# Linear attention with an RMS norm, then a two-layer token MLP: 512-token windows across batches in place of 576-token batches

## The chip, the cores and the metric

The kernel runs on one core of a Trainium2 chip. The metric is the device time of one execution in microseconds (us). The profile covers the same core: TensorE as two rows, PE for matmuls and PEld for weight loads; VectorE (DVE), ScalarE (ACT), GpSimd (POOL) and SyncE (SP). All of q, k, v and both weight matrices are loaded through POOL's DMA queue, which converts float32 to float16 on the way; the output leaves through SP's queue.

## The reference

```python
# q, k, v: (8, 8, 576, 64); w_in: (512, 2048); w_out: (2048, 512); alpha: (2048,)
kv  = np.einsum('bhsd,bhse->bhde', k, v)
out = np.einsum('bhsd,bhde->bhse', q, kv)
rms = np.sqrt(np.mean(out * out, axis=-1, keepdims=True) + 1e-06)
attn = out / rms * g_norm                                  # per head of 64
x = attn.transpose(0, 2, 1, 3).reshape(4608, 512)
h = x @ w_in
g = np.maximum(h, 0.0) + alpha * np.minimum(h, 0.0)
return g @ w_out                                           # (4608, 512) float32
```

The sum over tokens in `kv` does not depend on the order of the tokens, as long as k and v have the same one. In all later steps a token is a column (or a row of the output) on its own.

## The kernel before, in words

Heads are taken in four pairs j, so that two heads of 64 fill 128 partitions. A batch has 576 tokens: four full tiles of 128 and one of 64, whose other half is zeroed once per buffer (L82). There are three buffers each of k, v and q (`ksb`, `vsb`, `qsb`), tokens on partitions.

`load_heads` (L89) loads one tensor of one batch with five DMAs, a tile of 128 tokens each; every piece of a row that it reads is one head's 64 values. Batch 0 is loaded in two halves of four heads, so 30 DMAs; then come `w_in` in four quarters (L133), batch 1, `w_out` in four quarters (L142) and batch 2. All of them are issued by POOL in this order, and the identity matrix for the transposes is made on POOL too (in a library file, masks.py), after the first 30. Each later batch is loaded while the batch two before it is worked on.

Attention of one batch and one pair is four steps:
- `step_t`: five PE transposes of q (`qt_ps`, L180) and a DVE copy to `qt_sb` (L189).
- `step_kv`: five matmuls (`kv_ps`, L196) and a DVE multiplication by a mask that keeps the two heads apart (`kv_sb`, L204).
- `step_ot`: `ot_ps` = kv times q, two matmuls of 288 columns (L209); ACT squares it (`sq_sb`, L214), DVE copies it to `ot_sb` (L216).
- `step_ssq`: a matmul with the mask sums the squares of each head (`ssq_ps`, L222); ACT makes `lnv` = Ln (L227) and `rstd` = Exp (L232); DVE makes `xt` = `ot_sb` x g x `rstd` (L233).

`step_stream` puts them in the order ot(j-1), t(j), ssq(j-1), kv(j), so 16 steps per batch. `qt_ps` and `kv_ps` share one PSUM bank, `ot_ps` and `ssq_ps` one buffer of two banks.

`m1_group(b, g)` makes 128 of the 2048 hidden values for the 576 tokens of batch b: eight matmuls of 288 columns (L276) into `h_ps`, two buffers of two banks each; ACT makes `m_sb` = relu(-h) (L286), and DVE `gt` = h + (1 - alpha) x `m_sb` in float16 (L287). The output product (`y_mm`, L296) is 16 matmuls of 512 columns for each of 36 tiles of 128 tokens; ACT copies the result (`y_out`, L303) and SP stores it.

The order of each engine is the order in which the code is written (manual schedule). First all of batch 0's attention, then its 16 hidden groups, then the output of the first four tiles at once, in four accumulators (`ya` and `yb`, two banks each, in `h_ps`' buffers) with one attention step of batch 1 after each g. From then on, per batch b and g: a hidden group, some output matmuls of earlier tokens (four or five, so that a tile may end and the next begin in the middle of a run), one attention step of the next batch. These output tiles have one PSUM bank (`y_ps`). Batch 1 has no output work, as no complete tile is left. After batch 7 five tiles remain.

Of the kernel before, what the change touches and what calls it, by code (L numbers as in the profile page):

```python
# [9 lines left out]
FP32 = mybir.dt.float32  # L10
# [7 lines left out]
def kernel(  # L18
# [31 lines left out]
    qkv_p = ctx.enter_context(tc.tile_pool(name="qkv", bufs=1))  # L50
    attn_p = ctx.enter_context(tc.tile_pool(name="attn", bufs=2))
# [7 lines left out]
    ctx.enter_context(tc.manual_schedule(engines={ENG.PE, ENG.Activation, ENG.DVE, ENG.Pool, ENG.SP}))  # L59
# [13 lines left out]


# [3 lines left out]
    for i in range(NBUF):  # L78
        t = {}
        for nm in ("k", "v", "q"):  # L80
            t[nm] = qkv_p.tile([P, NT, H, D], FP16, name=f"{nm}sb{i}")
            nc.vector.memset(t[nm][REM:P, NFULL, :, :], 0.0)  # L82
        bufs.append(t)

    def load_heads(b, nm, h0, h1):
        t = bufs[b % NBUF][nm]
        for ti in range(NT):
            n = P if ti < NFULL else REM
            nc.gpsimd.dma_start(  # L89
                out=t[0:n, ti, h0:h1, :],  # L90
                in_=srcs[nm][b, h0:h1, ti * P : ti * P + n, :].rearrange("h s d -> s h d"),
            )
# [16 lines left out]
    ident = const_p.tile([P, P], FP32, name="ident")
    make_identity(nc, ident[:])  # L110
    ident16 = const_p.tile([P, P], FP16, name="ident16")
    nc.vector.tensor_copy(out=ident16[:], in_=ident[:])
    eps_t = const_p.tile([P, 1], FP32, name="eps_t")
    nc.vector.memset(eps_t[:], 1e-6)

    mask32 = const_p.tile([P, P], FP32, name="mask32")
    nc.vector.memset(mask32[:], 0.0)
    nc.vector.memset(mask32[0:64, 0:64], 1.0)
    nc.vector.memset(mask32[64:128, 64:128], 1.0)
    mask16 = const_p.tile([P, P], FP16, name="mask16")  # L120
    nc.vector.tensor_copy(out=mask16[:], in_=mask32[:])
# [8 lines left out]
    def load_w_in():  # L130
        for i in range(WQ):
            t = w_p.tile([P, NC, FW], FP16, name=f"w_in_sb{i}")
            nc.gpsimd.dma_start(  # L133
                out=t[:],
                in_=moe_w_in[:, i * FW : (i + 1) * FW].rearrange("(c p) f -> p c f", p=P),
            )
            w_in_sb.append(t)

    def load_w_out():
        for i in range(WQ):  # L140
            t = w_p.tile([P, GW, D_MODEL], FP16, name=f"w_out_sb{i}")
            nc.gpsimd.dma_start(  # L142
# [245 lines left out]
```

## Time and profile before

| | us |
|---|---|
| Median of 3 runs (378.38 to 378.71) | 378.6 |
| The profiled execution, whole | 378.55 |
| Its span in the profile | 376.4 |
| PE busy (2049 matmuls) | 300.3 |
| DVE busy | 175.1 |
| ACT busy | 167.9 |
| POOL busy | 116.4 |

In timelines and groups a row names the engine, the line of the code, the operation, output <- inputs, the shape (partitions x elements) and a count; what stands in brackets is the idle time just before it and what ended it. Matmuls are pipelined: a row's duration includes the drain, and the cost in a row of matmuls is the distance between starts. `<-issue` means that nothing in the profile explains the wait.

### The profile page before, as it was taken

Reading aid. Unit: us, or ns where it says so; the run is one execution under the profiler, and the core shown is the slowest. Engines: PE = TensorE matmul, PEld = TensorE weight load, DVE = VectorE, ACT = ScalarE, POOL = GpSimd, SP = SyncE. Lnnn points to the kernel's source line nnn. Section 1 sums busy time; section 2 is a strip of 40 time slices with the busy share of each in tenths; the row PEclk is TensorE's granted clock in tenths of the full one; section 3 lists DMA queues with packets and bytes.
Section 4 is the critical chain, followed back from the end, with each engine's and each line's share of the span. In section 5 each row is a group of like instructions: output and inputs, shape, how many; then the busy total and the mean of one; then the engine's idle time right before and its main releaser. Section 6 shows DMA issues by size and latency. Waiting matters only on the chain.

```text
span 376.4 us, 5119 instructions
## 1 busy us (share of the span) xinstructions
PE 300.3 (80%) x2049; PEld 191.0 (51%) x2049; DVE 175.1 (47%) x272; ACT 167.9 (45%) x261; POOL 116.4 (31%) x149
## 2 busy tenths in 40 slices
PE   0033489895886899979997889799978999799885
PEld 0022367443664555556665555566655555466432
DVE  2014348433776544546664454555654455344100
ACT  1003346245666354546664454546553445444211
POOL 8995947939308400290048000000000000000000
PEclk9999999998999999999999999999999999999999
DMA  9999999999909900298059401000000000010111
GB/s 59 81 101 197 154 205 161 154 92 128 174 0 86 132 30 28 42 152 81 29 58 162 56 28 57 28 28 30 30 29 28 30 28 30 28 57 28 50 63 57
DMA packets 122375, 28.13 MB, mean 75 GB/s; under 512 B 113632, under 2 KB 117744, under 8 KB 122352
## 3 DMA queue, kind: packets, MB, share of 16 engines
q0 software_dynamic: 116976, 18.36, 66.1%
q1 hardware_dynamic: 5376, 9.45, 6.7%
q8 instruction: 16, 0.26, 0.3%
q14 instruction: 7, 0.06, 0.0%
HBM read 36.71 MB, written 9.44 MB: 123 GB/s over the span
## 4 chain that ended last, share of the span: by engine, by line
PE 71%; ACT 13%; DVE 7%; POOL 6%; issue 3%; ACTq 0%; POOLq 0%
PE h_ps L276 30%; PE y_ps L296 29%; ACT y_sb L303 4%; ACT lnv L227 4%; DVE xt L233 3%; ACT rstd L232 3%; PE ot_ps L209 3%; PE qt_ps L180 2%; PE ssq_ps L222 2%; POOL ksb L89 2%; POOL vsb L89 2%; POOL qsb L89 2%; PE kv_ps L196 2%; DVE ot_sb L216 1%; ACT m_sb L286 1%
## 5 line engine op out<-in xcount | busy, mean ns | idle before, releaser
L276 PE MATMUL h_ps<-xt,w_in_sb 128*128 128x288 f16 x1024 | 149.6, 292 | 14.9 <-DVE xt L233 12.1
L287 DVE SCALAR_TENSOR_TENSOR gt<-m_sb,beta_sb,h_ps 128x576 f16<-128x576 f32 x128 | 104.0, 813 | 78.1 <-ACT m_sb L286 77.9
L296 PE MATMUL y_ps<-w_out_sb,gt 128*128 128x512 f16 x512 | 128.9, 379 | 13.6 <-ACT y_sb L303 13.6
L286 ACT ACTIVATE m_sb<-h_ps 128x576 f32<-128x576 f32 x128 | 83.0, 648 | 103.5 <-PE h_ps L276 103.5
L276 PEld LDWEIGHTS <-w_in_sb 128*128 128x128 f16 x1024 | 100.2, 100 | 45.0 <-issue 17.1
L296 PEld LDWEIGHTS <-gt 128*128 128x128 f16 x576 | 55.9, 98 | 61.9 <-issue 16.9
L89 POOL DMA_DIRECT2D ksb<-in_k_dram x45 | 37.0, 859 | 78.5 <-PE kv_ps L196 76.7
L233 DVE SCALAR_TENSOR_TENSOR xt<-ot_sb,g2col,rstd 128x576 f16<-128x576 f32 x32 | 26.2, 819 | 46.4 <-ACT rstd L232 46.4
L214 ACT ACTIVATE sq_sb<-ot_ps 128x576 f16<-128x576 f32 x32 | 20.8, 651 | 55.9 <-PE ot_ps L209 55.9
L89 POOL DMA_DIRECT2D vsb<-in_v_dram x45 | 37.0, 872 | 10.6 <-DMA w_out_sb<-in_moe_w_out_dram 6.1
L89 POOL DMA_DIRECT2D qsb<-in_q_dram x45 | 37.2, 905 | 0.2
L216 DVE COPY ot_sb<-ot_ps 128x576 f32<-128x576 f32 x32 | 24.2, 758 | 23.6 <-ACT sq_sb L214 23.6
L227 ACT ACTIVATE lnv<-ssq_ps,eps_t 128x576 f32<-128x576 f32 x32 | 23.7, 742 | 21.4 <-PE ssq_ps L222 21.4
L303 ACT COPY y_sb<-y_ps 128x512 f32<-128x512 f32 x32 | 18.7, 584 | 23.1 <-PE y_ps L296 23.1
L209 PE MATMUL ot_ps<-qt_sb,kv_sb 128*128 128x288 f16 x64 | 14.2, 306 | 12.2 <-DVE kv_sb L204 12.2
L232 ACT ACTIVATE rstd<-lnv 128x576 f32<-128x576 f32 x32 | 21.8, 682 | 1.0
L162 PE MATMUL alpha_ps<-ident,alpha_row 16*128 16x16 f32 x1 | 0.3, 281 | 23.6 <-POOL ident masks.py:199 23.6
L222 PE MATMUL ssq_ps<-sq_sb,mask 128*128 128x288 f16 x64 | 14.0, 302 | 5.7 <-DVE ot_sb L216 5.7
L189 DVE COPY qt_sb<-qt_ps 128x576 f16<-128x576 f16 x32 | 14.4, 451 | 4.8 <-PE qt_ps L180 4.8
L180 PEld LDWEIGHTS <-qsb 128*128 128x128 f16 x160 | 12.8, 105 | 7.4 <-issue 0.8
L196 PEld LDWEIGHTS <-ksb 128*128 128x128 f16 x160 | 12.6, 104 | 7.3 <-issue 0.9
L180 PE MATMUL qt_ps<-ident,qsb 128*128 128x128 f16 x160 | 15.6, 233 | 0.8 <-DVE beta_sb L168 0.8
(28 smaller groups left out, 69.6 us busy)
## 6 DMA issues: line engine op xcount, KB each, us to landing
out_dram<-y_sb SPq DMA_DIRECT2D x36, 256.0 KB, 2.0
ksb<-in_k_dram POOLq DMA_DIRECT2D x28, 128.0 KB, 4.5
vsb<-in_v_dram POOLq DMA_DIRECT2D x28, 128.0 KB, 5.9
qsb<-in_q_dram POOLq DMA_DIRECT2D x28, 128.0 KB, 5.6
w_in_sb<-in_moe_w_in_dram POOLq DMA_DIRECT2D x4, 512.0 KB, 8.2
w_out_sb<-in_moe_w_out_dram POOLq DMA_DIRECT2D x4, 512.0 KB, 10.3
ksb<-in_k_dram POOLq DMA_DIRECT2D x15, 64.0 KB, 3.3
vsb<-in_v_dram POOLq DMA_DIRECT2D x15, 64.0 KB, 3.3
```

Source lines behind the costliest of these rows:

```text
L89: nc.gpsimd.dma_start(out=t[0:n, ti, h0:h1, :], in_=srcs[nm][b, h0:h1, ti * P : ti * P + n, :].rearrange("h s d -> s h d"),)
L180: nc.tensor.matmul(out=qt_ps[:, t * P : (t + 1) * P], lhsT=qs[:, t, 2 * j : 2 * j + 2, :], rhs=ident16[:], is_transpose=True, start=(t == ...
L209: nc.tensor.matmul(out=ot_ps[:, i, 0:HS], lhsT=st["kv"][:], rhs=st["qt"][:, i * HS : (i + 1) * HS], start=True, stop=True,)
L216: nc.vector.tensor_copy(out=st["ot"][:], in_=ot_ps[:, :, 0:HS])
L227: nc.scalar.activation(out=lnv[:], in_=ssq_ps[:, :, 0:HS], func=AF.Ln, bias=eps_t[:], scale=inv_d,)
L232: nc.scalar.activation(out=rstd[:], in_=lnv[:], func=AF.Exp, bias=0.0, scale=-0.5)
L233: nc.vector.scalar_tensor_tensor(out=xts[b, j][:], in0=st["ot"][:], scalar=g2col[:], in1=rstd[:], op0=ALU.mult, op1=ALU.mult,)
L276: nc.tensor.matmul(out=h_ps[:, i, 0:HS], lhsT=w_in_blk(c, g), rhs=xts[b, c][:, i, :], start=(c == 0), stop=(c == NC - 1),)
L286: nc.scalar.activation(out=m_sb[:], in_=h_ps[:, :, 0:HS], func=AF.Relu, scale=-1.0)
L287: nc.vector.scalar_tensor_tensor(out=gt[:, o : o + S].rearrange("p (i s) -> p i s", i=2), in0=m_sb[:], scalar=beta_sb[:, g : g + 1], in1=h ...
L296: nc.tensor.matmul(out=y, lhsT=gts[bp][g][:, o : o + P], rhs=w_out_blk(g), start=(g == 0), stop=(g == NF - 1),)
L303: nc.scalar.copy(out=y_sb[:], in_=y)
```

## The change

Tokens are regrouped into nine windows of 512 columns, 36 tiles as before, whatever the batch borders. What was per batch (hidden groups, norm, `xt`) is now per window, with one PSUM bank per product.

- **Loads.** `load_main` brings tokens 0 to 511 of a batch with partition p holding tokens 4p to 4p+3, so that one piece of a row is four tokens of a head. It goes to a staging tile (`kst`, `vst`, `qst`, two buffers). `regroup` then copies it on chip into the layout that the matmuls read. `load_rem` loads the last 64 tokens as before. A batch takes six DMAs. Batch 0 comes in four head pairs. It is regrouped by DVE (k, q) and ACT (v), batch 1 by DVE, batches 2 to 7 by POOL. The token order within a batch is permuted thereby, and `y_out` stores each row to its place, with two DMAs for a tile that is cut.
- **Start.** Identity, masks and small constants are made ahead of the loads. `keep_warm` puts matmuls into PE's queue whose result nobody reads: ten first, two after each attention step of batch 0, one after the last.
- **PSUM.** `h_ps` has three buffers of one bank, `ot_ps` two, `ssq_ps` one, `qt_ps` and `kv_ps` one together, `y_ps` one.
- **Norm.** `xt` is made from `ot_ps` in PSUM; the copy to `ot_sb` is gone. Ln and Exp write the same tile.
- **Order.** In the first output block (window 0) the attention steps of window 1 begin at g = 6 and go two at a time from g = 10. Later, from window 2 on, every g has a hidden group, four output matmuls of the window before and an attention step of the window after, so that a tile ends at every fourth g. The last window's four tiles rotate through the banks of `h_ps`.

DVE's queue in the start, for the first pair and the second. Names with a number are tiles, `kst` and `qst` the staging tiles. Before, from the first `qt_sb`:

```order
L189 COPY qt_sb<-qt_ps 128x576
L204 TENSOR_TENSOR kv_sb<-kv_ps,mask_153 128x128
L216 COPY ot_sb<-ot_ps 128x576
L189 COPY qt_sb<-qt_ps 128x576
L233 SCALAR_TENSOR_TENSOR xt<-ot_sb,g2col,rstd 128x576
L204 TENSOR_TENSOR kv_sb<-kv_ps,mask_153 128x128
```

Now:

```order
L139 COPY ksb_119<-kst 128x2x4x64
L139 COPY qsb_123<-qst 128x2x4x64
L231 COPY qt_sb<-qt_ps 128x576
L245 TENSOR_TENSOR kv_sb<-kv_ps,mask_102 128x128
L139 COPY ksb_119<-kst 128x2x4x64
L139 COPY qsb_123<-qst 128x2x4x64
L231 COPY qt_sb<-qt_ps 128x576
L275 SCALAR_TENSOR_TENSOR xt<-ot_ps,g2col,rstd 128x512
L245 TENSOR_TENSOR kv_sb<-kv_ps,mask_102 128x128
```

The copy to `ot_sb` is gone; two regroups per pair stand ahead of the transposes' copy; `kv_sb` of the next pair still comes behind `xt`.

PE's queue at the end of the first output block, from the last `ot` product to the next hidden group (LDWEIGHTS rows are weight loads). Before, the last output matmuls lay between `ot` and `ssq`:

```order
L209 LDWEIGHTS kv_sb
L209 MATMUL ot_ps<-qt_sb,kv_sb 128x288
L296 LDWEIGHTS gt
L296 MATMUL ya<-w_out_sb_188,gt 128x512
L296 MATMUL yb<-w_out_sb_188,gt 128x512
L222 LDWEIGHTS mask_157
L222 MATMUL ssq_ps<-sq_sb,mask_157 128x288
L276 LDWEIGHTS w_in_sb_159
L276 MATMUL h_ps<-xt,w_in_sb_159 128x288
```

Now:

```order
L332 MATMUL yd<-w_out_sb_178,gt 128x512
L256 LDWEIGHTS kv_sb
L256 MATMUL ot_ps<-qt_sb,kv_sb 128x64
L256 LDWEIGHTS kv_sb
L256 MATMUL ot_ps<-qt_sb,kv_sb 128x448
L268 LDWEIGHTS mask_106
L268 MATMUL ssq_ps<-sq_sb,mask_106 128x512
L310 LDWEIGHTS w_in_sb_155
L310 MATMUL h_ps<-xt,w_in_sb_155 128x512
```

`ssq` now follows `ot` directly, and `ot` is split where the window crosses a batch. (In the rows before, repeated rows of the same kind are left out.)

The diff, cut to its core:

```diff
-    ps_h = ctx.enter_context(tc.tile_pool(name="psh", bufs=2, space=bass.MemoryType.PSUM))
+    ps_h = ctx.enter_context(tc.tile_pool(name="psh", bufs=3, space=bass.MemoryType.PSUM))
...
-    ps_b = ctx.enter_context(tc.tile_pool(name="psb", bufs=1, space=bass.MemoryType.PSUM))
+    ps_o = ctx.enter_context(tc.tile_pool(name="pso", bufs=2, space=bass.MemoryType.PSUM))
+    ps_q = ctx.enter_context(tc.tile_pool(name="psq", bufs=1, space=bass.MemoryType.PSUM))
...
-    def load_heads(b, nm, h0, h1):
-        t = bufs[b % NBUF][nm]
-        for ti in range(NT):
-            n = P if ti < NFULL else REM
-            nc.gpsimd.dma_start(
-                out=t[0:n, ti, h0:h1, :],
-                in_=srcs[nm][b, h0:h1, ti * P : ti * P + n, :].rearrange("h s d -> s h d"),
-            )
+    def load_main(b, nm, h0, h1):
+        st = stages.get((b, nm))
+        if st is None:
+            st = stage_p.tile([P, H, TPP, D], FP16, name=f"{nm}st", tag=f"{nm}st")
+            stages[b, nm] = st
+        nc.gpsimd.dma_start(
+            out=st[:, h0:h1, :, :].rearrange("p h t d -> p h (t d)"),
+            in_=srcs[nm][b, h0:h1, 0:MAIN, :].rearrange("h (p t) d -> p h (t d)", t=TPP),
+        )
+    def regroup(b, nm, h0, h1, eng=None):
+        dst = bufs[b % NBUF][nm][:, 0:TPP, h0:h1, :].rearrange("p t h d -> p h t d")
+        src = stages[b, nm][:, h0:h1, :, :]
+        if eng is nc.scalar:
+            nc.scalar.copy(out=dst, in_=src)
+        else:
+            (eng or nc.vector).tensor_copy(out=dst, in_=src)
+    def load_batch(b, names=("k", "v", "q")):
+        for nm in names:
+            load_rem(b, nm)
+            load_main(b, nm, 0, H)
+    def regroup_batch(b):
         for nm in ("k", "v", "q"):
-            load_heads(b, nm, 0, H)
+            regroup(b, nm, 0, H, nc.gpsimd)
...
+    for j in range(NPAIR):
+        for nm in ("k", "v", "q"):
+            load_main(0, nm, 2 * j, 2 * j + 2)
+            if j == 0:
+                load_rem(0, nm)
+    for i in range(WQ):
+        load_w_in(i)
+    load_batch(1, ("k",))
+    load_w_out(0)
+    load_w_out(1)
+    load_batch(1, ("v", "q"))
+    load_w_out(2)
+    load_w_out(3)
     load_batch(2)
+    regroup_batch(2)
+    def keep_warm(n):
+        ps = ps_y.tile([P, W], FP32, name="warm_ps", tag="y")
+        for i in range(n):
+            nc.tensor.matmul(out=ps[:], lhsT=mask16[:], rhs=warm16[:], start=True, stop=True)
+    keep_warm(10)
...
-        st["ot"] = attn_p.tile([P, 2, HS], FP32, name="ot_sb")
-        nc.vector.tensor_copy(out=st["ot"][:], in_=ot_ps[:, :, 0:HS])
...
         nc.vector.scalar_tensor_tensor(
-            out=xts[b, j][:],
-            in0=st["ot"][:], scalar=g2col[:], in1=rstd[:], op0=ALU.mult, op1=ALU.mult,
+            out=xts[w, j][:], in0=ot_ps[:], scalar=g2col[:], in1=rstd[:],
+            op0=ALU.mult, op1=ALU.mult,
         )
...
+    for j in range(NPAIR):
+        regroup(0, "k", 2 * j, 2 * j + 2)
+        regroup(0, "v", 2 * j, 2 * j + 2, nc.scalar)
+        regroup(0, "q", 2 * j, 2 * j + 2)
+        n = 3 if j == 0 else 4
+        for _ in range(n):
+            attn_step()
+            keep_warm(2)
+    while windows_done < 1:
+        attn_step()
+        keep_warm(1)
...
+    for nm in ("k", "v", "q"):
+        regroup(1, nm, 0, H)
...
     for g in range(NF):
-        for t in range(4):
-            y_mm(ys[t], t, g)
-        attn_step()
+        for a in range(TPW):
+            y_mm(ys[a], 0, a, g)
+        if g >= 6:
+            attn_step()
+        if g >= 10:
+            attn_step()
...
+    for w in range(1, NW):
+        if w + 2 < B:
+            load_batch(w + 2)
+            regroup_batch(w + 2)
+        y = None
+        for g in range(NF):
+            m1_group(w, g)
+            if w > 1:
+                a, part = divmod(g, TPW)
+                if part == 0:
+                    y = ps_y.tile([P, W], FP32, name="y_ps", tag="y")
+                for gg in range(part * TPW, (part + 1) * TPW):
+                    y_mm(y, w - 1, a, gg)
+                if part == TPW - 1:
+                    y_out(y, w - 1, a)
+            attn_step()
+        while windows_done < min(w + 2, NW):
+            attn_step()
+    for a in range(TPW):
+        y = ps_h.tile([P, W], FP32, name="y_ps", tag="h")
+        for g in range(NF):
+            y_mm(y, NW - 1, a, g)
+        y_out(y, NW - 1, a)
```

`m1_group(w, g)` is four matmuls of 512 columns for one window; `step_ot` makes one product per batch that the window touches.

More of the change, by code (lines that the diff above doesn't have):

```diff
@@ L109 @@
[L109 to L120, printed above, removed]
@@ L209, in step_ot @@
             nc.tensor.matmul(
[L210 to L226 removed]
+                out=ot_ps[:, n0 - w * W : n1 - w * W], lhsT=kvs[b, j][:],
@@ new lines, in step_ot, with step_ssq @@
+                rhs=qts[b, j][:, n0 - b * S : n1 - b * S], start=True, stop=True,
+            )
+            n0 = n1
+        sq = attn_p.tile([P, W], FP16, name="sq_sb")
+        nc.scalar.activation(out=sq[:], in_=ot_ps[:], func=AF.Square)
+        ots[w, j] = (ot_ps, sq)
+    def step_ssq(w, j):
+        ot_ps, sq = ots.pop((w, j))
+        ssq_ps = ps_q.tile([P, W], FP32, name="ssq_ps", tag="q")
+        nc.tensor.matmul(out=ssq_ps[:], lhsT=mask16[:], rhs=sq[:], start=True, stop=True)
+        rstd = attn_p.tile([P, W], FP32, name="rstd")
```

266 lines of the change are left out of this document (124 added, 142 removed).

## The prediction

> **What bounds the kernel now.** I read the page's shares and chain first, then the stages as time windows, then PE's waits.
>
> ```profile
> PE 300.3 (80%) x2049; PEld 191.0 (51%) x2049; DVE 175.1 (47%) x272; ACT 167.9 (45%) x261; POOL 116.4 (31%) x149
> ...
> PE 71%; ACT 13%; DVE 7%; POOL 6%; issue 3%; ACTq 0%; POOLq 0%
> ```
>
> PE ends the work, but 29% of the chain is not PE. The windows (us; busy time and count of each engine, clock, DMA share, GB/s) are my stages A to F: start; first hidden block; first output block; second batch; steady state; tail.
>
> ```profile
> 0.00:48.50 48.50, 11.49 (x63) 7.38 (x64) 12.10 (x32) 9.58 (x13) 42.85 (x62) 1.00 1.45 121
> 48.50:65.87 17.37, 17.37 (x122) 13.03 (x122) 11.48 (x15) 9.77 (x15) 10.30 (x13) 1.00 1.79 182
> 65.87:91.00 25.13, 19.01 (x122) 9.80 (x120) 10.28 (x18) 9.96 (x16) 19.20 (x24) 1.00 1.79 115
> 91.00:121.19 30.19, 23.90 (x190) 17.44 (x190) 21.06 (x32) 18.98 (x30) 13.13 (x17) 0.94 1.07 97
> 121.19:351.00 229.81, 210.12 (x1474) 135.66 (x1474) 119.40 (x175) 115.95 (x182) 30.93 (x38) 1.00 0.40 51
> 351.00:376.40 25.40, 18.38 (x82) 7.73 (x80) 0.81 (x1) 3.65 (x7) 0.00 (x0) 1.00 0.17 63
> ```
>
> PE is idle for 37 of A's 48.5 us, and for 39 us more in all the rest. Its waits say on what:
>
> ```profile
> PE alpha_ps L162 <- POOL ident masks.py:199: 23.6, 1, 23.6
> PE y_ps L296 <- ACT y_sb L303: 13.6, 17, 1.0
> PE h_ps L276 <- DVE xt L233: 12.1, 7, 1.9
> PE h_ps L276 <- ACT y_sb L303: 2.5, 1, 2.5
> ```
>
> First the identity, made on POOL behind 30 load issues; then the single `y_ps` bank; then the last `xt` of each batch.
>
> **Prices.** One step of the steady state: transposes, hidden product, output product, next attention step.
>
> ```profile
> 201.50 0.44 PE L180 MATMUL qt_ps<-ident,qsb 128*128 128x128 f16 x5
> ...
> 201.78 1.14 PE L276 MATMUL h_ps<-xt,w_in_sb 128*128 128x288 f16 x8
> ...
> 202.75 1.24 PE L296 MATMUL y_ps<-w_out_sb,gt 128*128 128x512 f16 x5
> ...
> 203.83 0.44 PE L196 MATMUL kv_ps<-vsb,ksb 128*128 128x128 f16 x5
> ```
>
> From start to start: 0.28 for five transposes, 0.97 for eight 288-column matmuls, 1.08 for five of 512, so 0.216 each. Per token 288 and 512 columns cost the same (0.121/288 = 0.42 ns, 0.216/512 = 0.42 ns): halving the matmul count saves no PE time. The gain must come from waits. ACT and DVE durations:
>
> ```profile
> L287 DVE SCALAR_TENSOR_TENSOR gt<-m_sb,beta_sb,h_ps 128x576 f16<-128x576 f32 x128 | 104.0, 813 | 78.1 <-ACT m_sb L286 77.9
> L286 ACT ACTIVATE m_sb<-h_ps 128x576 f32<-128x576 f32 x128 | 83.0, 648 | 103.5 <-PE h_ps L276 103.5
> L233 DVE SCALAR_TENSOR_TENSOR xt<-ot_sb,g2col,rstd 128x576 f16<-128x576 f32 x32 | 26.2, 819 | 46.4 <-ACT rstd L232 46.4
> L227 ACT ACTIVATE lnv<-ssq_ps,eps_t 128x576 f32<-128x576 f32 x32 | 23.7, 742 | 21.4 <-PE ssq_ps L222 21.4
> L303 ACT COPY y_sb<-y_ps 128x512 f32<-128x512 f32 x32 | 18.7, 584 | 23.1 <-PE y_ps L296 23.1
> L232 ACT ACTIVATE rstd<-lnv 128x576 f32<-128x576 f32 x32 | 21.8, 682 | 1.0
> L189 DVE COPY qt_sb<-qt_ps 128x576 f16<-128x576 f16 x32 | 14.4, 451 | 4.8 <-PE qt_ps L180 4.8
> ```
>
> On ACT, L303 (512 columns) against L286 (576) gives 64 ns for 64 columns, so at 512 columns relu and square cost 0.58, Ln 0.68, Exp 0.62. DVE has no such pair: `gt` and `xt` lie between 0.72 (all of it scales) and 0.81 (nothing does), and I take 0.75, as most of ACT's time scales too. `xt` reading PSUM instead of `ot_sb` is bounded by `gt` (reads PSUM, 0.813) and the old `xt` (0.819): no change. The removed `ot_sb` copy is DVE time, worth something only where PE waits for it.
>
> **A, the start (48.5 -> 29.0).**
>
> ```profile
> 1.25 3.75 POOL L89 DMA_DIRECT2D ksb<-in_k_dram  x5 [0.80 <-POOLq L372]
> ...
> 22.69 0.46 POOL masks.py:197 MEMSET ident<- 128x128 f32 x1
> 23.23 0.29 POOL masks.py:199 TENSOR_SCALAR_AFFINE_SELECT ident<-ident 128x128 f32<-128x128 f32 x1
> ...
> 24.67 0.69 PE L180 MATMUL qt_ps<-ident,qsb 128*128 128x128 f16 x5 [0.82 <-DVE beta_sb L168]
> ...
> 29.18 0.64 PE L222 MATMUL ssq_ps<-sq_sb,mask 128*128 128x288 f16 x2 [1.00 <-DVE ot_sb L216]
> ...
> 32.41 0.66 PE L209 MATMUL ot_ps<-qt_sb,kv_sb 128*128 128x288 f16 x2 [2.07 <-DVE kv_sb L204]
> ```
>
> The identity moves ahead of the loads (0.75 us, loads start at 2.0). The first head pair needs six DMAs, the sixth issued at 2.0 + 5 x 0.75 = 5.75. Landing:
>
> ```profile
> qsb<-in_q_dram POOLq DMA_DIRECT2D x15, 64.0 KB, 3.1
> ...
> 12.00:24.00 12.00, 0.28 (x1) 0.28 (x2) 0.38 (x4) 0.00 (x0) 11.93 (x19) 1.00 1.31 83
> ...
> 28.00:30.00 2.00, 1.00 (x8) 0.66 (x7) 1.12 (x2) 0.48 (x2) 2.00 (x4) 1.00 1.24 206
> ```
>
> So it lands at about 9; with a regroup of 0.4 (by L189: 512 elements) the transposes start at 9.5, not 24.67. The half loads of batch 0 moved 83 GB/s (second window), the weights with their long rows 206 (third); four-token rows lie between, and I take 180. A batch is 1.77 MB in fp16 (14.2 MB of loads over 8), both weights 4.2. Batch 0 is then in at 15, and the last quarter of `w_out`, 6 MB behind it, at about 46; the output block asks for its third quarter at 50. Even at 83 for batch 0 pair 3 is in at 23, when it is due, and the weights come 3 us late at worst. So the loads' gain in bandwidth is worth nothing by itself; what counts is the first pair.
>
> From transposes to sum of squares took 4.5. Of the 1.00 of idle ahead of `ssq` I take 0.85 as the wait for `ot_sb`, now gone; the filler matmuls put 0.3 in its place: 13.5. Each further pair: `ssq` to the next `ot` (Ln, Exp, `xt`, `kv_sb`) took 3.23; 0.06, 0.06 and 0.07 for shorter operations and 0.23 for one warm matmul in place of two cold ones make it 2.8. Then `ot`, two fillers, transposes, two fillers: 0.22 + 0.43 + 0.28 + 0.43 = 1.36, more than the square behind `ot` takes (0.22 + 0.2 + 0.58). Period 4.2, before 5.4. After the third pair no transposes stand between. 13.5 + 2 x 4.2 + 2.8 + 1.0 = 25.7; `xt` ends 2.6 later, without `kv_sb` and `ot`: 28.3. The regroups of k and q (0.8 a pair) stand on DVE between `kv_sb` and the transposes' copy and overrun the 0.65 of PE work that covers them by 0.2: 29.0. v's regroup goes through ACT while PE does the transposes. The fillers sit mostly in waits; where these close they cost 0.43 a step. Ends of the range: 27 (regroups free), 33.5 (rival 1).
>
> **B and C (42.5 -> 39.6).** Hidden products: 61 x 0.216 = 13.2, now warm. The output block: 64 x 0.216 = 13.8; a fourth accumulator waits 0.7 for the last `gt`; attention on PE 8 x 0.28 + 8 x 0.216 = 3.97. Its steps now start at g = 6 and go two at a time, so every `ot` comes 1.36 after the preceding `ssq` and needs 2.8: 3 x 1.45 lost, 0.8 more for the last square. Then the hidden products of the next window need a bank that `yb` holds: ACT does Ln, Exp and two copies first, 1.8 + 1.2 after `ssq`, 2.8 of it idle. DVE's three regroups of batch 1 stand ahead of this block's first `qt_sb` copy, but between 0.4 (L189) and 1.6 each (the same rate over 2048 elements) they end before g = 6 asks for it. Sum 26.4, worse than 25.13. B + C = 39.6, ending at 68.6.
>
> **D (30.2 -> 28.3).**
>
> ```profile
> 99.35 0.41 PE L222 MATMUL ssq_ps<-sq_sb,mask 128*128 128x288 f16 x2
> ...
> 103.39 0.42 PE L209 MATMUL ot_ps<-qt_sb,kv_sb 128*128 128x288 f16 x2 [1.14 <-DVE kv_sb L204]
> ...
> 105.88 0.41 PE L222 MATMUL ssq_ps<-sq_sb,mask 128*128 128x288 f16 x2
> ```
>
> `kv_sb` stands behind `xt` and a `gt` on DVE, before and after: 4.04 becomes 4.0, plus `ot`, two groups and transposes 2.2: period 6.2 (6.53 before). First `ssq` 6.1, third 18.5, fourth 23.6, last `xt` 26.5. The slow clock after C's wait stays:
>
> ```profile
> 91.00 2.08 PE h_ps L276 x8
> ```
>
> 2.08 and 1.47 in place of 0.98 for its first groups, and the small products with them: 1.8. The Trainium skill (TensorE: Matmul & The Clock Gate, Part 1) lets PE fall to half clock only after a whole idle window of some 3.4 us; this row follows an idle of 2.51, so the measurement decides; by the rule D would be 1.8 shorter.
>
> **E (229.8 -> 224.5).** Seven windows of 128 x 0.216 = 27.65: 193.6. Attention: 5 x 3.97 + 1.73 = 21.6, less 0.65 for matmuls counted in D. The boundary wait:
>
> ```profile
> 197.13 0.41 PE L222 MATMUL ssq_ps<-sq_sb,mask 128*128 128x288 f16 x2
> ...
> 200.18 0.40 PE L276 MATMUL h_ps<-xt,w_in_sb 128*128 128x288 f16 x2 [1.90 <-DVE xt L233]
> ```
>
> 3.05 from `ssq` to the release by the last `xt`; 0.19 less now, 2.86, of which `ssq` and three matmuls cover 0.86: 2.0 at five boundaries, 10.0. This wait the change leaves where it was. The y switch goes to 0: its copy (0.2 + 0.58 + 0.05) lies under an attention step and a whole hidden group (1.14); uncovered it costs 0.7. A window that crosses a batch splits its `ot` product in two, 28 times in all; if a weight load (191.0/2049 = 0.09) shows behind each, that is 2.6 us, which goes into the range. ACT and DVE work per window (19 and 18 us of 33.7) stays under PE.
>
> **F (25.4 -> 18.0).**
>
> ```profile
> 369.17 3.61 PE L296 MATMUL y_ps<-w_out_sb,gt 128*128 128x512 f16 x16 [0.72 <-ACT y_sb L303]
> 372.87 0.59 ACT L303 COPY y_sb<-y_ps 128x512 f32<-128x512 f32 x1 [3.75 <-PE y_ps L296]
> ```
>
> Four tiles, not five, in rotating banks: 64 x 0.216 = 13.8. From the end of the last issue (369.17 + 16 x 0.216 = 372.6) to 376.4 it is 3.8, and the last tile's output is now two DMAs on SP, 0.35 more (an estimate, half of a POOL issue). Elsewhere SP's 56 in place of 36 output DMAs have a window of 33 us for six or seven.
>
> Sum: 29.0 + 39.6 + 28.3 + 224.5 + 18.0 = 339.4. The profiled run took 378.55 with a span of 376.4, 2.15 outside, and lies 0.05 under the median: **342 us**.
>
> **Rivals.** 1. *Regroups collide with load issues.* If each of the six k and q regroups of pairs 1 to 3 waits out one POOL issue (0.75), the transposes come 1.5 later in three periods: 346.5. For it: POOL is busy 42.85 of A's 48.5. Against: no row before shows DVE waiting for POOL's issues. The Trainium skill (SBUF — State Buffer, "Who interferes with whom") says a DVE copy between SBUF tiles in a two-port mode and GpSimd block each other fully; no row of this trace tests it.
> 2. *POOL's regroup becomes the bound (slower).* From batch 2 on, three copies of 2048 elements per partition run on POOL behind six issues. By the two rows of POOL work on 128 elements (0.29 and 0.46) one costs 4.6 to 7.4; I take 5. With issues at 0.86, a batch is then 20 us, under a window's 33.7. But batch 7 is due at about 232: starting at 49, six batches of 5.2 + 3x reach 268, where the gain is used up, from x = 10.4 on; at 11 the time is about 380.
> 3. *Every y switch still waits*: 28 x 0.7 = 20, so 361. Against it the cover of 1.14.
> 4. *C and D don't stall as worked out* (DVE serves `kv_sb` in time): 8 less, 334.
>
> **How the numbers follow.** Forecast 0.64; rival 1 0.18; rival 4 0.08; rival 3 0.06; rival 2 0.03; no gain 0.01. The forecast's own range, 335 to 350, comes from a start of 27 to 33.5 and stalls of C and D of half to full size plus small split matmuls; with rivals 1 and 4, and half of 3, 332 to 355. 0.2% is what a measurement can tell: faster 0.96, same 0.01, slower 0.03.
>
> **What would show it.** First transposes at 9 to 10 us; first hidden matmuls at 26 to 28; `y_ps <- y_sb` waits near 0 in the steady state; window period 33 to 34; one wait for `xt` of about 1.9 a window; stalls for `kv_sb` in the output block. Wrong, if POOL's copies exceed 10 us or PE waits inside a window.

## The result and the profile after

The changed kernel takes 340.35 us (median of 4 runs, 339.78 to 340.94), the kernel before 378.51 (378.38 to 378.71). The ratio is 0.8991, 95% interval 0.8971 to 0.9012. Forecast were 342 us, 332 to 355. The profiled execution took 339.78 with a span of 338.0.

The page of the changed kernel, busy time of each engine:

```profile
PE 300.1 (89%) x1614; PEld 143.8 (43%) x1614; DVE 159.7 (47%) x272; ACT 174.8 (52%) x293; POOL 84.3 (25%) x89
```

PE's busy time reads the same as before (300.3), with 435 matmuls fewer, but it does not hold the same work. 14.3 us of it are the filler matmuls:

```profile
L201 PE MATMUL warm_ps<-warm,mask 128*128 128x512 f16 x41 | 14.3, 454 | 2.3 <-DVE warm L95 2.3
```

The run without them (e5) shows the gain more plainly: PE is busy for 295.6 us of its 340.7 there and idle for 45.1, against 76.1 idle of 376.4 before. So 31.0 of its 35.7 us are idle time of PE; where the other 4.7 of busy time went is not traced. Where the gain of the changed kernel lies shows in the same stages A to F, now with their new borders (columns as before):

```profile
0.00:28.52 28.52, 18.23 (x93) 7.76 (x94) 12.22 (x37) 11.07 (x17) 21.42 (x34) 0.94 1.18 156
28.52:41.68 13.16, 13.16 (x61) 5.96 (x61) 10.49 (x15) 8.96 (x15) 4.81 (x7) 1.00 1.41 198
41.68:68.13 26.45, 18.95 (x117) 9.34 (x116) 8.99 (x17) 9.26 (x16) 13.33 (x12) 0.98 1.22 150
68.13:94.88 26.75, 20.71 (x119) 10.07 (x119) 16.68 (x28) 16.95 (x30) 18.29 (x17) 0.95 0.95 138
94.88:319.40 224.52, 215.28 (x1162) 104.57 (x1162) 110.80 (x176) 125.66 (x211) 26.44 (x21) 1.00 0.30 53
319.40:338.00 18.60, 13.80 (x64) 6.07 (x62) 0.54 (x1) 2.92 (x5) 0.00 (x0) 0.97 0.30 71
```

| Stage | before | predicted | after | gain |
|---|---|---|---|---|
| A, start | 48.50 | 29.0 | 28.52 | 19.98 |
| B + C, first hidden and output block | 42.50 | 39.6 | 39.61 | 2.89 |
| D, second window | 30.19 | 28.3 | 26.75 | 3.44 |
| E, steady state | 229.81 | 224.5 | 224.52 | 5.29 |
| F, tail | 25.40 | 18.0 | 18.60 | 6.80 |
| Sum | 376.4 | 339.4 | 338.0 | 38.4 |

What PE still waits for, in us, times, and the longest:

```profile
PE h_ps L310 <- DVE xt L275: 12.4, 7, 1.8
PE ot_ps L256 <- DVE kv_sb L245: 11.5, 9, 1.3
PE h_ps L310 <- ACT y_sb L339: 2.4, 1, 2.4
...
PE qt_ps L222 <- DVE qsb L139: 2.2, 2, 1.8
```

The rows for the identity (23.6 before) and for `y_sb` at the y switches (13.6) are gone. The wait for the last `xt`, once per window, has stayed (12.1 before), and the waits for `kv_sb` lie in A, C and D.

### The profile page after: what moved, and what is told of

It reads as the page before. It is cut to its first block, busy times and chain, and to the rows that moved or that the text cites. A ratio compares the mean times of both kernels' runs of the same rounds, so it can differ in the third digit from the quotient of the medians.

```text
span 338.0 us, 4258 instructions
## 1 busy us (share of the span) xinstructions
PE 300.1 (89%) x1614; PEld 143.8 (43%) x1614; DVE 159.7 (47%) x272; ACT 174.8 (52%) x293; POOL 84.3 (25%) x89
## 4 chain that ended last, share of the span: by engine, by line
PE 80%; ACT 9%; DVE 5%; POOL 2%; DMA 2%; issue 1%; POOLq 0%; ACTq 0%
PE h_ps L310 34%; PE y_ps L332 33%; DVE xt L275 3%; ACT rstd L270 3%; ACT rstd L273 3%; PE ot_ps L256 3%; PE qt_ps L222 3%; PE kv_ps L237 2%; PE ssq_ps L268 2%; DMA qst<-in_q_dram 2%; ACT y_sb L339 1%; ACT m_sb L317 1%; DVE gt L319 1%; PE yd L332 1%; PE ya L332 1%
## 5 line engine op out<-in xcount | busy, mean ns | idle before, releaser
L310 PE MATMUL h_ps<-xt,w_in_sb 128*128 128x512 f16 x576 | 147.6, 382 | 14.8 <-DVE xt L275 12.4
L319 DVE SCALAR_TENSOR_TENSOR gt<-m_sb,beta_sb,h_ps 128x512 f16<-128x512 f32 x144 | 107.4, 746 | 97.0 <-ACT m_sb L317 95.1
L317 ACT ACTIVATE m_sb<-h_ps 128x512 f32<-128x512 f32 x144 | 85.3, 594 | 83.7 <-PE h_ps L310 83.2
L310 PEld LDWEIGHTS <-w_in_sb 128*128 128x128 f16 x576 | 54.0, 98 | 57.7 <-issue 6.1
L275 DVE SCALAR_TENSOR_TENSOR xt<-ot_ps,g2col,rstd 128x512 f16<-128x512 f32 x36 | 27.0, 751 | 46.4 <-ACT rstd L273 46.4
L262 ACT ACTIVATE sq_sb<-ot_ps 128x512 f16<-128x512 f32 x36 | 21.5, 597 | 35.7 <-PE ot_ps L256 35.5
L270 ACT ACTIVATE rstd<-ssq_ps,eps_t 128x512 f32<-128x512 f32 x36 | 24.8, 688 | 14.4 <-PE ssq_ps L268 14.4
L256 PE MATMUL ot_ps<-qt_sb,kv_sb 128*128 128x512 f16 (+7 forms) x64 | 15.2, 292 | 11.5 <-DVE kv_sb L245 11.5
L273 ACT ACTIVATE rstd<-rstd 128x512 f32<-128x512 f32 x36 | 22.7, 629 | 1.1
L201 PE MATMUL warm_ps<-warm,mask 128*128 128x512 f16 x41 | 14.3, 454 | 2.3 <-DVE warm L95 2.3
L256 PEld LDWEIGHTS <-kv_sb 128*128 128x128 f16 x64 | 6.2, 97 | 21.9 <-DVE kv_sb L245 15.7
L128 POOL DMA_DIRECT2D ksb<-in_k_dram x8 | 5.7, 713 | 37.5 <-PE kv_ps L237 35.7
```

What stands on the lines that cost most here:

```text
L256: nc.tensor.matmul(out=ot_ps[:, n0 - w * W : n1 - w * W], lhsT=kvs[b, j][:], rhs=qts[b, j][:, n0 - b * S : n1 - b * S], start=True, stop=True,
L262: nc.scalar.activation(out=sq[:], in_=ot_ps[:], func=AF.Square)
L270: nc.scalar.activation(out=rstd[:], in_=ssq_ps[:], func=AF.Ln, bias=eps_t[:], scale=inv_d,)
L273: nc.scalar.activation(out=rstd[:], in_=rstd[:], func=AF.Exp, bias=0.0, scale=-0.5)
L275: nc.vector.scalar_tensor_tensor(out=xts[w, j][:], in0=ot_ps[:], scalar=g2col[:], in1=rstd[:], op0=ALU.mult, op1=ALU.mult,)
L310: nc.tensor.matmul(out=h_ps[:], lhsT=w_in_blk(c, g), rhs=xts[w, c][:], start=(c == 0), stop=(c == NC - 1),)
```

## The experiments

Each was made from the changed kernel unless it says otherwise. Its time is a median. The kernel before took 378.51 to 379.09 beside them.

### e1: the identity behind the loads again

```diff
-    make_identity(nc, ident[:])          # ahead of all loads
+    make_identity(nc, ident[:])          # behind the loads of batch 0
```

> The changed kernel (340.4 us) with one thing undone: the identity is made on POOL behind the 15 loads of batch 0, and its float16 cast stands behind the zeroing on DVE. Theory (the start was bound by the identity, not by the data): the transposes start at about 12.5 to 13.5 instead of 8.4, the other three pairs' data is there by then, and the whole is 4 to 5 us slower, 344.5 to 345.5. Rival (the start was bound by the loads' bandwidth, the identity only happened to be last): first transposes still at about 8 to 9, 340 to 341.

345.22 us (344.61 to 345.47), ratio to before 0.9119, interval 0.9105 to 0.9132. PE's longest wait and the first transposes:

```profile
PE alpha_ps L205 <- POOL ident masks.py:199: 6.0, 1, 6.0
...
13.67 0.72 PE L222 MATMUL qt_ps<-ident,qsb 128*128 128x128 f16 x5 [0.73 <-DVE qsb L135]
```

The transposes start 5.3 later (8.38 in the changed kernel), the total rises by 4.9 and the window period stays at 33.60. The place of the identity sets the start.

### e2: rows of one token loaded as before, no regroup

```diff
-    load_main(0, nm, 2 * j, 2 * j + 2); load_rem; regroup(...)
+    load_heads(0, nm, 2 * j, 2 * j + 4)     # five DMAs, straight into ksb, vsb, qsb
-    two output DMAs for a cut tile
+    nc.sync.dma_start(out=out[n0 : n0 + P, :], in_=y_sb[:])
```

> The changed kernel with the loads of the kernel before: five DMAs per tensor and batch, 64-value rows straight into the matmuls' tiles, batch 0 in two halves of four heads, no staging, no regroup, output tiles stored in one piece. Identity first, fillers and windows stay. Theory: only the first pair's lateness counts. 15 issues of 0.72 from 1.4, landing 3 later: first transposes at 14.5 instead of 8.4, the third pair waits 2 more for the second half: 8 us slower, 348; steady state as it is. Rival (four-token rows free bandwidth that the rest of the kernel needs): 355 or more, with waits for loads or weights after 40 us.

347.47 us (347.17 to 348.08), ratio 0.9183, interval 0.9169 to 0.9197. A wait for loads appears, and the first hidden product with all `xt`, which stands at 28.52 in the changed kernel, comes later:

```profile
PE qt_ps L196 <- DMA qsb<-in_q_dram: 7.9, 6, 4.9
...
36.16 13.32 PE L284 MATMUL h_ps<-xt,w_in_sb 128*128 128x512 f16 x61 [1.36 <-DVE xt L249]
```

The start is 7.6 longer, and the window period behind it is the same, 33.60. So the new loads with their regroups are worth 7.6 us, all in stage A: no later product waits for a load. The total rises by less, 7.1: the second window is 0.7 longer, as PE's clock was halved for longer there (last section), and the rest behind it 1.1 shorter (242.0 for 243.1); the output tiles, stored in one piece, are the likely reason, not tried alone. Of the wait, 4.9 fall on the first q tile of the first pair and 3.0 on five later waits, two of them, 1.1 together, in the third pair, so it is not only the first pair that matters.

### e3: the kernel before with the identity ahead of the loads

```diff
+    make_identity(nc, ident[:])          # now ahead of the 30 loads of batch 0
     srcs = {"q": q, "k": k, "v": v}
```

> The kernel before (378.5 us) with one change: the identity is made on POOL ahead of the loads. Theory: its first transposes move from 24.7 to about 15 (15 issues of 0.72, landing 3), then the third pair waits for the second half (25.5): first hidden products with all of xt at 39 to 41 instead of 48.5, so 7.5 to 9.5 us faster, 369 to 371. Rival (the data was as late as the identity): within 2 us of 378.5.

369.81 us (369.33 to 370.21), ratio 0.9769, interval 0.9753 to 0.9786. This single move gains 8.75 of the 38 us. What is late next is the load:

```profile
PE qt_ps L180 <- DMA qsb<-in_q_dram: 12.0, 8, 8.9
```

So the two parts hide each other: 8.75 for the identity with the old loads, 4.9 with the new ones (e1).

### e4: the last norm of a window one group earlier

```diff
             m1_group(w, g)
+            if w > 1 and g < 2:
+                attn_step()
             ...                                  # output matmuls
-            attn_step()
+            if windows_done < w + 2:
+                attn_step()
```

> The changed kernel with the attention steps of windows 3 and later advanced: in groups 0 and 1 of each window from the second on, a second attention step stands between the hidden and the output products, so that the last norm of the next window is done at g = 13 and not at g = 15. Theory: the wait of the first hidden group for the last xt (1.84 at five boundaries, 2.0 with the drain) is an exposed latency and goes away: 9 to 10.5 us faster, 330 to 331.5. Rival (what is saved at the border is paid inside the window, as DVE and ACT are pressed there): 338 to 341, with new waits of PE inside the windows.

335.71 us (335.05 to 336.19), ratio 0.8869, interval 0.8852 to 0.8885. The gain is 4.6, half of what was expected:

```profile
PE kv_ps L237 <- DVE qt_sb L231: 3.5, 5, 0.7
PE h_ps L310 <- DVE xt L275: 3.2, 2, 1.8
```

The wait for `xt` fell from 12.4 to 3.2, but a new one of 0.7 appeared in each of five windows. With the steps t and kv only one output chain apart, the copy to `qt_sb` stands on DVE behind `gt` of the group before, and `kv_ps`, which has the same PSUM bank, waits for it. That takes back 3.2 of the 9.2; longer waits for the square, for q and for `kv_sb` take 1.1 more.

### e5: no filler matmuls

```diff
-        for i in range(n):
+        for i in range(0):      # keep_warm issues nothing; its results are read by nobody
```

> The changed kernel (340.4 us) without the filler matmuls. Theory: in the start they lie in waits and change the attention chain by less than 1 us either way (0.43 per step against the same products at half clock); what they buy is a warm PE for the first hidden products, whose first 4 us would run at half speed: 1 to 3 us slower, 341.4 to 343.4. Rival (they stand in the way of the chain and buy nothing): 338.5 to 340.

343.22 us (342.42 to 343.68), ratio 0.9059, interval 0.9041 to 0.9077: 2.9 more than with them. The first hidden block, and the window over its first matmuls (the last three columns are clock, DMA share, GB/s):

```profile
28.93 15.23 PE L311 MATMUL h_ps<-xt,w_in_sb 128*128 128x512 f16 x61 [0.94 <-DVE xt L276]
```

```profile
28.90:31.00 2.10, 2.07 (x5) 0.69 (x5) 0.75 (x1) 0.60 (x1) 0.59 (x2) 1.00 1.26 206
```

Stage A itself is only 0.4 longer. The 61 matmuls take 15.23 instead of 13.33 (the same row in e8 below). The first of them run at some 0.42 us each, half the usual pace, until about 33 us. The clock column reads 1.00 there, so the pace shows that PE is at full speed here with the fillers and not without them, but not by which mechanism.

### e6: matmuls of 256 columns

```diff
-            nc.tensor.matmul(out=h_ps[:], ..., rhs=xts[w, c][:], ...)
+        for i in range(2):                      # around the loop over c
+            nc.tensor.matmul(out=h_ps[:, i*256:(i+1)*256], ..., rhs=xts[w, c][:, i*256:(i+1)*256], ...)
```

> The changed kernel with each hidden product of 512 columns made as two of 256 (576 matmuls and weight loads more, same columns, same bank). Theory (columns cost the same in any size, 0.42 ns): PE's row rate gives 0 to 0.003 us per extra matmul, 340 to 342. Rival (the larger column block is itself what saves PE time): each extra matmul costs 0.02 or more, 352 or more.

344.03 us (343.41 to 345.68), ratio 0.9091, interval 0.9069 to 0.9113. The excess over the expected 340 to 342 is mostly in the border wait:

```profile
92.89 0.49 PE L311 MATMUL h_ps<-xt,w_in_sb 128*128 128x256 f16 x3
95.55 0.71 PE L311 MATMUL h_ps<-xt,w_in_sb 128*128 128x256 f16 x5 [2.17 <-DVE xt L275]
```

With the halves in the outer loop, only three half matmuls stand ahead of the one that needs the last `xt`, where three whole ones stood; the wait is 0.32 longer (2.17 for 1.85). The window period rose by 0.48 to 34.08, so 64 more matmuls per window cost 0.16, or 2.5 ns each. Columns, and hardly the number of matmuls, are what PE pays for. The second window took 27.49, 0.74 more than in the changed kernel, as PE's clock was halved for longer there (last section).

### e7: the norm reads a copy of `ot` again

```diff
-        ots[w, j] = (ot_ps, sq)
+        nc.vector.tensor_copy(out=ot_sb[:], in_=ot_ps[:])
+        ots[w, j] = (ot_sb, sq)
```

> The changed kernel with the copy of ot from PSUM to SBUF on DVE put back, and the scaling made from it. Theory: DVE has slack in the steady state (16 of 32 us busy); the 0.7 shows only in the start, where it stands ahead of the next pair's regroups and transposes' copy (up to 0.9 for three pairs), and a little in the second window: 1.5 to 4 us slower, 342 to 344.5. Rival (the 36 copies, 25 us of DVE time, were on the path): 352 or more.

345.45 us (344.21 to 348.33), ratio 0.9137, interval 0.9107 to 0.9168: 5.1 more, above the expected 342 to 344.5.

```profile
PE qt_ps L222 <- DVE qsb L139: 6.3, 4, 1.8
...
32.74 13.33 PE L312 MATMUL h_ps<-xt,w_in_sb 128*128 128x512 f16 x61 [1.36 <-DVE xt L277]
```

The start is 4.2 longer, about 1.05 per pair, as the copy stands on DVE ahead of the next pair's regroups. The steady period is again 33.60: there the 24 us of extra DVE work cost nothing. The profile is of the fastest of six runs (344.21), so the rest of the 5.1 lies in their spread, which no trace explains.

### e8: the attention steps of the first output block spread out

```diff
-        if g >= 6: attn_step()
-        if g >= 10: attn_step()
+    at = {1: 1, 2: 1, 3: 2, 4: 2, 7: 2, 8: 2, 11: 2, 12: 2, 15: 2}
+        for _ in range(at.get(g, 0)): attn_step()
```

The regroup of batch 1 starts with q instead of k.

> The changed kernel with the attention steps of window 1 placed otherwise in the first output block: q of batch 1 regrouped first, steps from g = 1 on, and three g between each sum of squares and the next ot product, in place of none. Theory: the three waits of ot for kv_sb (1.25 each, 1.45 with the drain) are there only because the steps start at g = 6 and go in pairs; they vanish: 3.5 to 4.5 us faster, 336 to 337. Rival (the block is bound by its output products and the last copies): within 1 us of 340.4.

335.90 us (335.42 to 336.03), ratio 0.8866, interval 0.8851 to 0.8881: 4.4 less.

```profile
PE ot_ps L256 <- DVE kv_sb L245: 7.9, 7, 1.3
...
28.34 13.33 PE L310 MATMUL h_ps<-xt,w_in_sb 128*128 128x512 f16 x61 [1.36 <-DVE xt L275]
```

Of the waits for `kv_sb`, 3.6 are gone, nearly all of stage C's. They came from when the steps are called.

### e9: in window 1, the attention step ahead of relu and `gt`

```diff
-            m1_group(w, g)
+            m1_mm(h_ps, w, g, range(NC))
+            if w == 1: attn_step()
+            m1_evac(h_ps, w, g)
             ...
-            attn_step()
+            if w > 1: attn_step()
```

> Edit: in window 1 alone (the second batch's window, 68.13 to 94.88 in the changed kernel) the attention step of a group is called after the group's four hidden matmuls and before its relu and gt; in the changed kernel it is called behind them. Nothing else moves. Theory (the pair period of 5.92 us there is a chain, not work: kv_sb, qt_sb, Ln and Exp stand behind a relu or a gt that is itself waiting for hidden products; 16 + 5 + 5 + 1 + 1 matmuls of a pair alone would be about 4.9 us): with the step's evacuations ahead of the group's own, PE waits less for kv_sb, the pair period falls to 5.0 to 5.4 and the stretch by 2 to 3.5 us; 337 to 338.5 us. Rival (the period is the work of ACT and DVE in these four groups, 4 x 0.59 + 0.6 + 1.37 on ACT, and the order only moves the waiting from kv_sb to the relu's): the period stays at 5.8 to 6.0 and the time at 340 to 341.

338.45 us (337.88 to 339.77), ratio 0.8935, interval 0.8913 to 0.8958: 1.9 less. The pair period fell only from 5.91 to 5.65, and the wait for `kv_sb` from 1.29 to 1.02. What stands ahead of `kv_sb` now:

```profile
76.21 0.44 PE L237 MATMUL kv_ps<-vsb,ksb 128*128 128x128 f16 x5
...
76.93 0.75 DVE L275 SCALAR_TENSOR_TENSOR xt<-ot_ps,g2col,rstd 128x512 f16<-128x512 f32 x1 [0.72 <-ACT rstd L273]
...
77.60 0.74 DVE L319 SCALAR_TENSOR_TENSOR gt<-m_sb,beta_sb,h_ps 128x512 f16<-128x512 f32 x1
...
78.25 0.28 DVE L245 TENSOR_TENSOR kv_sb<-kv_ps,mask 128x128 f16<-128x128 f32 x1
```

`kv_ps` is complete at about 76.65, but DVE waits in its order for Exp, then makes `xt` and a `gt`, and only then `kv_sb`. The theory was half right: the order matters, but `kv_sb` also stands behind the norm of the pair before. Calling kv ahead of ssq was not tried.

### e10: e8, e4 with the order of e9, and e9, together

```diff
-            m1_group(w, g)
+            m1_mm(h_ps, w, g, range(NC))
+            if w == 1 or g < 2: attn_step()
+            m1_evac(h_ps, w, g)
             ...
-            attn_step()
+            if w > 1 and windows_done < w + 2: attn_step()
```

and the placing of e8.

> Edit: three placements together. (a) the steps of the first output block spread as in e8 (that run alone: 335.90, 4.4 less than the changed kernel). (b) as in e4, the last square sum, Ln/Exp and xt of a window come one group earlier, before the first output chain of the window, but the attention step of the first two groups of every window is now called between the group's hidden matmuls and its relu and gt, so that the qt_sb copy no longer stands behind gt (in e4 that was a new wait of 0.7 us per window for kv_ps). (c) the same order for all groups of window 1. Theory (the costs of these waits add up, and e4's remaining loss was the order on DVE): 4.4 from (a), 6 to 9 from (b) (e4 gave 4.6 with a qt_sb wait of 3.5 in all, and left 3.2 of the xt wait), 2 to 3.5 from (c), so 340.4 less 12.4 to 17 = 323.5 to 328 us, with the window period at 31.9 to 32.4 instead of 33.60. Rival (evacuations moved ahead of relu and gt only move the wait to the hidden products' banks or to gt): the parts of (b) and (c) are given back, and it is e8's 335.9 less e4's 4.6 = 331 us or more.

**324.65 us** (324.10 to 325.35), ratio 0.8570, interval 0.8551 to 0.8589: 15.7 us less than the changed kernel, and the fastest version run here. Its windows for the steady state and its waits:

```profile
89.38:302.97 213.59, 213.59 (x1157) 104.20 (x1157) 111.29 (x176) 122.68 (x210) 34.00 (x29) 1.00 0.34 60
```

```profile
PE h_ps L310 <- DVE xt L275: 2.9, 2, 1.6
```

PE is busy for all of the 213.59 us. The border wait remains only at the start and before window 2, and e4's new wait for `qt_sb` is gone, so it was the order on DVE. The first transposes of two windows that follow each other start at 121.19 and 152.79, 31.60 apart. The gain is more than the 11 or so that e8, e4 and e9 gave alone (4.4, 4.6 and 1.9).

### e11: regroups of batches 3 to 7 on DVE

```diff
-            regroup_batch(w + 2)                       # POOL
+            if w + 2 < B and g in (9, 11, 13):
+                regroup(w + 2, {9: "k", 11: "v", 13: "q"}[g], 0, H)   # DVE
```

> Edit: the regroup copies of batches 3 to 7 (15 copies of 128x2048 fp16) go from POOL (1.89 us each) to DVE (0.69 us each in batch 1), called behind the groups 9, 11 and 13 of the window in which the loads were issued. Theory (POOL's copies are off every path, and DVE has room in the window: 47% busy): POOL busy falls by 28 us, DVE rises by about 10, the time stays at 339.5 to 341.5, and the gt rows keep their 746 ns. Rival 1 (POOL's copies slow DVE while they run, as the stretched regroups at the start beside POOL's DMA issues might mean): gt's mean falls visibly below 746 ns and the time by 0.5 to 2 us, 338.5 to 340. Rival 2 (DVE in its order waits for the loads, or a late gt holds up PE): a wait of PE for gt, 0.3 to 0.7 us for each copy that decides, 5 to 10 us in all, 345 to 350.

340.65 us (340.33 to 341.04), ratio 0.8989, interval 0.8971 to 0.9007: no difference clear of the spread (339.78 to 340.94 for the changed kernel). POOL's busy time fell, DVE's rose, and `gt` kept its 746 ns:

```profile
PE 301.4 (89%) x1614; PEld 144.6 (43%) x1614; DVE 167.9 (50%) x287; ACT 174.8 (52%) x293; POOL 56.6 (17%) x74
...
L319 DVE SCALAR_TENSOR_TENSOR gt<-m_sb,beta_sb,h_ps 128x512 f16<-128x512 f32 x144 | 107.4, 746 | 90.2 <-ACT m_sb L317 88.4
```

POOL's copies are off every path, and `gt` got no shorter without them; DVE has room for them too.

## Why the prediction was right

**A (29.0, measured 28.52).** The chain was as worked out, but its first link holds two misses that cancel. The rows of the changed kernel's PE:

```profile
8.38 0.45 PE L222 MATMUL qt_ps<-ident,qsb 128*128 128x128 f16 x5 [1.82 <-DVE qsb L139]
...
12.63 0.48 PE L222 MATMUL qt_ps<-ident,qsb 128*128 128x128 f16 x5 [0.39 <-DVE qsb L139]
...
13.38 0.38 PE L268 MATMUL ssq_ps<-sq_sb,mask 128*128 128x512 f16 x1
...
16.18 0.39 PE L256 MATMUL ot_ps<-qt_sb,kv_sb 128*128 128x512 f16 x1 [1.28 <-DVE kv_sb L245]
```

The transposes start 1.1 sooner than the 9.5 forecast, as the loads land sooner. The first `ssq` comes at 13.38 all the same (13.5), since it stands in PE's order behind the second pair's transposes, and these wait for their own load, as the regroup ahead of them on DVE shows:

```profile
12.28 0.29 DVE L139 COPY qsb<-qst 128x512 f16<-128x512 f16 x1 [1.38 <-DMA qst<-in_q_dram]
```

That this second wait ends where the forecast had put `ssq` is luck. From there `ssq` to `ot` takes 2.80 (2.8), the next two periods 4.49 and 4.17 (4.2), the last `ssq` is at 25.92 (25.7), and the last `xt` releases 2.60 later (2.6). The 0.7 for regroups that overrun their cover was too much by about 0.5. e1 and e2 show that identity and loads both set this stage; e7 gives the removed copy 1.05 per pair, where the working had 0.85 once and little afterwards, so its size was underrated, within a sum that came out. (e7 puts the copy among the regroups; among the old loads it was not tried.)

**B and C (39.6, measured 39.61).** 61 products in 13.2 (13.16). C's losses stand as forecast (the forecast's figures, in brackets, hold the drain of the matmul before, some 0.16, which the trace counts as busy): waits for `kv_sb` of 1.25 three times (1.45), 0.69 for the square (0.8), 0.66 for the last `gt` in two parts (0.7), 2.40 for `yb`'s bank (2.8). e8 took most of the first away, as the forecast's cause for it, the steps going two at a time, would have it.

**D (28.3, measured 26.75).** This is the term most off. Two pair periods of 5.91, not 6.2, and 4.77 from the third `ssq` to the fourth, not 5.1, make 0.9 of the 1.55. The slow clock is the next part:

```profile
68.13 1.86 PE L310 MATMUL h_ps<-xt,w_in_sb 128*128 128x512 f16 x4 [2.40 <-ACT y_sb L339]
...
71.83 0.44 PE L237 MATMUL kv_ps<-vsb,ksb 128*128 128x128 f16 x5 [0.27 <-DVE qt_sb L231]
```

From 68.13 to the end of the second group at 71.56 (71.83 less 0.27 idle) it is 3.43; at the full clock two groups, five transposes and the last drain take 2 x 0.864 + 0.28 + 0.16 = 2.17. So the penalty was 1.3, not 1.8. The rest, 0.1, is not traced. The penalty's size is partly luck: in e11, where the pair period is the same, the clock stayed halved for longer at this place (last section) and the stage took 27.73.

**E (224.5, measured 224.52).** The terms came out one by one. PE is busy for 215.3 (214.6 forecast) and idle for 1.85 at a border (2.0), but these two are the same drain, counted on either side. The row of three matmuls below is 0.81 long for starts 0.216 apart, so 0.16 of it is the drain. Without five of these PE's work is 214.5; with it a wait is 2.01, from 126.48, where the fourth matmul would start, to 128.49. The 28 split `ot` products, for which the range held up to 2.6, show no extra time. The rows of one border, and the group of the output products with its idle time in the last column:

```profile
125.83 0.81 PE L310 MATMUL h_ps<-xt,w_in_sb 128*128 128x512 f16 x3
128.49 0.38 PE L310 MATMUL h_ps<-xt,w_in_sb 128*128 128x512 f16 x1 [1.85 <-DVE xt L275]
...
L332 PE MATMUL y_ps<-w_out_sb,gt 128*128 128x512 f16 x512 | 128.8, 379 | 0.0
```

The y switch costs nothing, as the cover of 1.14 promised, so rival 3 is out. No run puts the old order of the y switches or the old windows back: that the 13.6 us of `y_ps` waits are gone is read from these rows. The statement that fewer, wider matmuls save PE no time is borne out by e6; PE's 300.1 does not test it, as the fillers are in it.

**F (18.0, measured 18.6).** The last tile's two stores take longer on SP than the 0.35 extra that was estimated. First the changed kernel, then the kernel before:

```profile
333.29 0.58 ACT L339 COPY y_sb<-y_ps 128x512 f32<-128x512 f32 x1 [2.91 <-PE y_ps L332]
333.90 1.11 SPq L351 DMA_DIRECT2D out_dram<-y_sb  x2
```

```profile
373.48 0.33 SPq L304 DMA_DIRECT2D out_dram<-y_sb  x1
```

1.11 in place of 0.33 is 0.8 more, 0.4 more than the forecast's extra, and makes that much of the 0.6 by which F is over. From the copy's end, 333.87 to 338.0 is 4.13, where it was 373.46 to 376.4, 2.94.

**Rivals.** Rival 2 rested on 4.6 to 7.4 us for a POOL copy; it takes 1.89 (row below), far under the 10.4 from which it would decide, and e11 shows it off the path. Rival 1 exists in a small form (last section): two of six regroups are stretched, by 0.3 and 0.6, and no period of A is 1.5 longer. Rival 4 was wrong about C, and right about D only as far as the 0.9 above.

## What to carry to other kernels

Add up PE's busy time first, and leave out products that nobody reads: here it is 300 us before and 296 without the fillers (e5), so little but waits could be won, and each stage was forecast within 1.6 us by finding the wait that ends last in it. When a product's operand comes from a chain over several engines, look at what stands ahead of each link on the in-order engines; calling the same steps at other places (spread out, a group earlier, or between a group's matmuls and their evacuation) was worth 15.7 us together (e10). Parts of a change that remove two causes of the same delay must be undone together and alone, since each hides the other (8.75 us and 4.9 us for the same move).

## What the runs showed of the hardware

**POOL's copy.** 2048 fp16 elements per partition take 1.89 us on POOL and 0.69 on DVE; the rows on 128 elements that the forecast scaled up to 4.6 and 7.4 (0.29 and 0.46, of other operations) were no measure for it.

```profile
L139 POOL COPY ksb<-kst 128x2048 f16<-128x2048 f16 x6 | 11.4, 1893 | 18.2 <-DMA kst<-in_k_dram 18.2
...
L139 DVE COPY ksb<-kst 128x2048 f16<-128x2048 f16 x1 | 0.7, 687 | 0.0
```

**DVE copies beside POOL's DMA issues.** The regroups of batch 0, 512 elements each, run, up to the third pair, while POOL issues loads without a break. The changed kernel's DVE and POOL timelines, then the group of the same copies of v on ACT:

```profile
6.69 0.28 DVE L139 COPY ksb<-kst 128x512 f16<-128x512 f16 x1
...
10.35 0.56 DVE L139 COPY ksb<-kst 128x512 f16<-128x512 f16 x1
...
16.04 0.86 DVE L139 COPY ksb<-kst 128x512 f16<-128x512 f16 x1
```

```profile
6.43 0.78 POOL L122 DMA_DIRECT2D vst<-in_v_dram  x1
...
9.98 0.81 POOL L122 DMA_DIRECT2D kst<-in_k_dram  x1
...
15.76 1.03 POOL L122 DMA_DIRECT2D kst<-in_k_dram  x1
```

```profile
L137 ACT COPY vsb<-vst 128x512 f16<-128x512 f16 x4 | 2.4, 612 | 4.3 <-DMA vst<-in_v_dram 4.3
```

The two stretched copies end at 10.91 and 16.90, each 0.11 or 0.12 behind the end of the issue beside them (10.79, 16.79). The first copy, begun 0.26 into its issue, is not stretched. ACT's copies beside the same issues keep 0.61. In e5 to e11 copies of k or q that were stretched lie the same way, with up to 0.79 and ends about 0.1 us behind an issue's end. The Trainium skill (SBUF — State Buffer, "Who interferes with whom") says that a DVE copy in a two-port mode and GpSimd lock each other out for a whole instruction and that ACT waits for neither. The trace agrees on ACT and on the wait; it differs in that a copy can run inside the first half microsecond of an issue, so no lock spans the whole of an issue here. Whether the copies ran in a two-port mode, no row shows. The most that one copy lost is 0.58. What the loss is worth in the total was not tried.

**The clock.** After the idle of 2.40 ahead of 68.13 the granted clock is halved, as the column ahead of the last two of this window of the changed kernel shows. Behind it stands the same place in e11, also after an idle of 2.40, where it stays halved for more than 5 us:

```profile
68.13:70.00 1.87, 1.87 (x6) 0.75 (x6) 0.00 (x0) 0.93 (x2) 1.40 (x1) 0.50 1.37 255
```

```profile
68.34:73.80 5.46, 5.46 (x21) 2.64 (x21) 1.81 (x4) 2.11 (x4) 0.88 (x1) 0.50 1.36 203
```

The idle of 1.85 at 128.49 was followed by matmuls at full speed (the next matmul there starts 0.21 later). But in stage A of the changed kernel the clock was halved too, after an idle of only 1.82 (ahead of 8.38) and some 0.9 us of work with the clock column at 1.00:

```profile
9.50:12.30 2.80, 2.74 (x10) 0.95 (x9) 0.78 (x3) 0.88 (x2) 2.80 (x5) 0.50 1.31 164
```

So the length of the last idle alone does not decide, and what does is not shown. The Trainium skill (TensorE: Matmul & The Clock Gate, Part 1), already set against the first case in the prediction, asks for more idle time than 2.40 or 1.82, and these measurements decide against it too.
